# LayerNorm rows transposed by the DMA crossbar instead of TensorE, from the fifth tile on

## The chip, the cores and the metric

The kernel runs on one core of one Trainium2 chip. A core has five engines with a queue each: TensorE (PE, with its weight loads shown apart as PEld), VectorE (DVE), ScalarE (ACT), GpSimd (POOL) and SyncE (SP). SP computes nothing here: it issues every DMA of the kernel, in order, and 16 DMA engines carry them out. The metric is the device time of one execution in microseconds; lower is better.

## The reference

Two layer kinds alternate, each twice, on one sequence of 2048 rows of 512 (bf16). A is sliding-window attention with 32 heads of 16 and a window of 256; B is an MLP with an inner width of 1792.

```python
def _A_ref(x, wqkv, wo):
    H = 32; Dh = D // H; W = 256
    q, k, v = split((x @ wqkv))                    # heads of 16
    scores = einsum("bhqd,bhkd->bhqk", q, k) * (Dh ** -0.5)
    mask = (i - j >= 0) & (i - j < W)
    p = softmax(where(mask, scores, -1e9))
    return einsum("bhqk,bhkd->bhqd", p, v).reshape(B, S, D) @ wo

def _B_ref(x, w1, b1, w2, b2):
    return gelu(x @ w1 + b1) @ w2 + b2

x = x + _A_ref(_layernorm(x), A_wqkv, A_wo)
x = x + _B_ref(_layernorm(x), B_w1, B_b1, B_w2, B_b2)
x = x + _A_ref(_layernorm(x), A_wqkv, A_wo)
x = x + _B_ref(_layernorm(x), B_w1, B_b1, B_w2, B_b2)
```

The LayerNorm has no weights: it subtracts the row's mean and divides by the square root of the variance plus 1e-5.

## The kernel before, in words

The sequence is cut into 16 tiles of 128 rows. The two passes over the layers are numbered through: `tau` runs from 0 to 31, and tile `tau % 16` of the residual `X` stays in on-chip memory all the time. All weights are loaded once at the start. Two tiles make a block `b` of attention (16 blocks over both passes).

What happens to one block:

- `lnq(b)` takes the LayerNorm of its two tiles into `xnTA` (layer 0), transposed, so that the row's 512 channels lie on partitions, and projects Q. `kv(b)` projects K and V from the same `xnTA`. Both are planned ahead of the block's attention: `lnq` two blocks ahead, `kv` one.
- `attention(b)` makes 8 x 2 visits. A visit multiplies K and Q of four heads in four row groups of PE (line 643), takes the exponential on ACT from PSUM into `E` (656), and masks it on DVE or POOL (661, 669). After every second pair of visits the products with V are accumulated (699), evacuated into `OD` by DVE or ACT, and divided by the softmax denominator.
- The division goes through DMA: `Dc` collects the denominators out of `OD` (716), DVE takes the reciprocal `Rc` (719), `scr_r` stores it in DRAM (721), `Rn` reads it back broadcast to all rows (723), four copies move the odd heads inside `OD` (726), and POOL or DVE multiplies into `OT` (729, 732). All seven DMAs of such a round are issued by SP. There are 64 rounds.
- `outproj` multiplies by Wo, adds to `X` (562), and takes the LayerNorm of layer 1 into `xnTB`.
- `mlp(J)` serves a job of two or four tiles from `xnTB`. Six of 14 inner chunks are evacuated by DVE first (786) and put through the gelu in pairs (789); the other eight go through ACT straight from PSUM (798). Then W2 and the second residual follow. In the second pass each finished tile is stored to the output (811). A job is let in `GLAG` = 26 visits after its tiles' block.

`layernorm` (line 508) is where the change acts. DVE takes the statistics (515, 517), POOL the reciprocal root (519, 522), DVE writes `xn` (525). Then the rows have to be turned:

- as it is before: four PE transposes into one PSUM bank (537), and an evacuation into `xnTA` or `xnTB` by DVE (line 502 within `evac`) or ACT (line 504), whichever the planner finds free first;
- the other branch: one `dma_start_transpose` issued on SP (530), which writes `xnTA` or `xnTB` directly.

The order of the instructions on each engine is fixed when the program is built. `_Plan` (168) is a list scheduler: every operation has an engine or alternatives, a cost in ns, a priority and the data that it reads and writes; PSUM banks come from pools (`"o"` is banks 6 and 7, for projections, PV, transposes and most outputs). For a DMA the plan has two numbers, the time for which SP is busy issuing (`issue`) and the time to landing (`dur`); for the transposing DMA they are `TRI` = 500 and `TRD` = 4300 ns. `_Sched` (20) then emits the operations in that order with semaphore waits. DMAs use eight semaphores in turn, and each waits until the previous one on its semaphore has landed:

```python
        if dma:
            assert eng == "sp"
            counter = "spdma%d" % (self.dma_rr % self.N_DMA_SEMS)
            self.dma_rr += 1
            inc = 16
            prev = self.cnt_val[counter]
            if prev > 0:
                need(counter, prev)
```

Of the kernel before, what the change touches and what calls it, by code (L numbers as in the profile page):

```python
# [330 lines left out]
def bass_interleave_layers__sliding_block__dense_activation_gelu__prompt_kernel(  # L331
# [39 lines left out]
    GLAG = 26  # L371
    MP1, MP2, QP, KP = 5.0, 255.0, 110.0, 140.0
    PVLAG = 1
    NPT = 1000
    TRD, TRI = 4300.0, 500.0
    PG = 2
    PREP = 0.0
# [19 lines left out]
    with ExitStack() as kctx:  # L397
# [73 lines left out]
        def dma(fn, writes, reads=(), dur=2200.0, prio=0.0, issue=330.0):  # L471
            add("sp", fn, dur, reads=reads, writes=writes, prio=prio, dma=True, geo=issue)
# [35 lines left out]
        def layernorm(tau, layer, dst, dcol, dname, prio):  # L508
# [19 lines left out]
                reads=["X%d" % t, "mv%d" % k, "rs%d" % k], writes=["xn%d" % s], prio=prio)  # L528
            if NPT <= tau + 100 * layer:
                dma(lambda e, B: e.dma_start_transpose(dst[:, :, dcol : dcol + P], xn[:, s, :]),  # L530
# [342 lines left out]
```

## Time and profile before

| | |
|---|---|
| median of three runs | 560.25 us (557.84 to 560.73) |
| the profiled execution's own time | 560.25 us |
| its span in the profile | 558.5 us |
| granted TensorE clock, mean | 0.976 of full speed |
| PE busy | 497.5 us (89%) |
| ACT busy | 476.9 us (85%) |
| DVE busy | 386.7 us (69%) |
| POOL busy | 281.3 us (50%) |
| DMA engines busy, mean share (SP's queue) | 14.4% |

Busy is the time in which an engine carries out an instruction. Matmuls are pipelined and their ends are modelled, so PE's busy time reads higher than its real work. An operation in a group is written out<-in with its line; the idle time given with a group is that of its engine just before it, with what ended it. SPq stands for SP's instruction queue. The chain that ended last is followed back from the last instruction, at each step to what released it.

### The profile page before, as it was taken

How to read it: one execution, taken by the hardware profiler on the slowest of the kernel's cores; microseconds unless marked ns; L12 is line 12 of the kernel's file. 1: busy time of each engine (PE TensorE's matmuls, PEld its weight loads, DVE VectorE, ACT ScalarE, POOL GpSimd, SP SyncE). 2: the span in 40 equal slices, each digit the busy share in tenths (PEclk: the TensorE clock that was granted, in tenths of full speed). 3: DMA queues.
4: the chain of work that ended last, by engine and by line, in shares of the span. 5: the costliest groups of instructions: out<-in, count | busy, mean ns of one | idle time of the engine just before them, and what ended most of it. 6: DMA issues, size and time to landing. Idle time of an engine off the chain costs nothing.

```text
span 558.5 us, 12849 instructions
## 1 busy us (share of the span) xinstructions
PE 497.5 (89%) x5008; PEld 238.5 (43%) x5008; DVE 386.7 (69%) x769; ACT 476.9 (85%) x708; POOL 281.3 (50%) x470
## 2 busy tenths in 40 slices
PE   3885689999979999888999999899999999878997
PEld 2543245445434443434334443444434543333553
DVE  5899688696879567946588667986787666735131
ACT  2699789999979999977989999899997999887532
POOL 6467564483765465722576456743564356421010
PEclk9999679999979999999999999999999999989999
DMA  8901111010111101110111101110111001111100
GB/s 276 289 18 34 29 33 36 16 35 26 32 33 31 32 7 35 30 33 26 32 27 37 30 18 33 31 32 16 41 46 47 25 23 41 50 32 35 51 21 28
DMA packets 37103, 24.44 MB, mean 44 GB/s; under 512 B 16305, under 2 KB 36530, under 8 KB 37042
## 3 DMA queue, kind: packets, MB, share of 16 engines
q1 hardware_dynamic: 37042, 23.62, 14.4%
q8 instruction: 39, 0.64, 0.5%
q14 instruction: 22, 0.18, 0.1%
HBM read 16.26 MB, written 2.62 MB: 34 GB/s over the span
## 4 chain that ended last, share of the span: by engine, by line
PE 35%; ACT 25%; DMA 15%; DVE 12%; SPq 8%; issue 3%; POOL 2%; DVEq 0%; POOLq 0%
PE ps L553 26%; ACT E L656 17%; SPq L726 6%; DMA Dc<-OD 6%; DMA Rn<-scr_r 5%; PE ps L643 5%; DMA scr_r<-Rc 4%; PE ps L699 3%; DVE E L661 3%; ACT gT L798 2%; ACT gT L789 2%; PE ps L537 1%; DVE KT L597 1%; ACT OD L504 1%; DVE gT L786 1%
## 5 line engine op out<-in xcount | busy, mean ns | idle before, releaser
L656 ACT ACTIVATE E<-ps 128x768 bf16<-128x768 f32 (+2 forms) x512 | 357.3, 785 | 28.0 <-PE ps L643 25.9
L669 POOL TENSOR_SCALAR_AFFINE_SELECT E<-E 128x512 bf16<-128x512 bf16 x216 | 161.6, 749 | 138.1 <-ACT E L656 136.8
L661 DVE TENSOR_TENSOR E<-E,mask 128x512 bf16<-128x512 bf16 x195 | 99.0, 510 | 39.2 <-ACT E L656 37.5
L553 PE MATMUL ps<-W_sb,gT 128*128 128x512 bf16 x448 | 121.7, 382 | 0.0
L553 PE MATMUL ps<-xnTB,W_sb 128*128 128x512 bf16 (+1 forms) x560 | 116.4, 345 | 3.4 <-DVE gT L786 2.2
L643 PE MATMUL ps<-QT,KT 32*128 32x384 bf16 (+2 forms) x1024 | 86.9, 328 | 19.3 <-ACT E L656 18.4
L553 PE MATMUL ps<-xnTA,Wqkv_sb 128*128 128x256 bf16 x512 | 72.5, 282 | 2.8 <-ACT xnTA L504 0.7
L553 PEld LDWEIGHTS ps<-xnTB,W_sb 128*128 128x128 bf16 x560 | 51.0, 99 | 47.5 <-issue 6.1
L643 PEld LDWEIGHTS ps<-QT,KT 32*128 32x128 bf16 x1024 | 25.8, 91 | 96.4 <-ACT E L656 81.8
L562 DVE TENSOR_TENSOR X<-X,ps 128x512 bf16<-128x512 bf16 x64 | 43.3, 677 | 31.2 <-PE ps L553 30.8
L798 ACT ACTIVATE gT<-ps,b1T 128x512 bf16<-128x512 f32 (+1 forms) x92 | 48.4, 587 | 12.3 <-PE ps L553 12.3
L699 PE MATMUL ps<-E,Va 128*17 128x128 bf16 (+1 forms) x1920 | 53.6, 254 | 5.3 <-DVE E L661 1.2
L553 PEld LDWEIGHTS ps<-W_sb,gT 128*128 128x128 bf16 x448 | 37.2, 98 | 47.5 <-issue 19.8
L553 PEld LDWEIGHTS ps<-xnTA,Wqkv_sb 128*128 128x128 bf16 x512 | 45.9, 100 | 21.3 <-issue 4.8
L665 POOL TENSOR_SCALAR_AFFINE_SELECT E<-E 128x512 bf16<-128x512 bf16 x61 | 39.8, 654 | 20.4 <-ACT E L656 20.1
L699 PEld LDWEIGHTS ps<-E,Va 128*17 128x17 bf16 x1920 | 39.0, 93 | 25.3 <-issue 10.9
L729 POOL TENSOR_TENSOR OT<-OD,Rn 128x256 bf16<-128x256 f32 x35 | 26.6, 761 | 39.6 <-DMA Rn<-scr_r 37.0
L515 DVE BATCH_NORM_STATS2 stat<-X 128x6 f32<-128x512 bf16 x64 | 43.0, 678 | 0.7
L597 DVE TENSOR_TENSOR KT<-ps,parmask 128x1024 bf16<-128x1024 f32 x32 | 38.8, 1213 | 6.5 <-PE ps L553 6.3
L537 PE MATMUL ps<-ident,xn 128*128 128x128 bf16 x256 | 26.1, 228 | 18.5 <-DVE xn L525 13.3
L519 POOL TENSOR_SCALAR veps<-statmv 128x1 f32<-128x1 f32 x64 | 15.2, 240 | 53.2 <-DVE statmv L517 53.0
L522 POOL TENSOR_TENSOR rstd<-veps,mhalf 128x1 f32<-128x1 f32 x64 | 38.3, 600 | 3.3
(44 smaller groups left out, 408.0 us busy)
## 6 DMA issues: line engine op xcount, KB each, us to landing
Rn<-scr_r SPq DMA_DIRECT2D x64, 128.0 KB
OD<-OD SPq DMA_DIRECT2D x256, 16.0 KB
W_sb<-in_B_w_dram SPq DMA_DIRECT2D x2, 1792.0 KB
out_dram<-X SPq DMA_DIRECT2D x16, 128.0 KB
Wqkv_sb<-in_A_wqkv_dram SPq DMA_DIRECT2D x3, 512.0 KB
X<-in_A_x_dram SPq DMA_DIRECT2D x1, 1024.0 KB
Dc<-OD SPq DMA_DIRECT2D x64, 8.0 KB
scr_r<-Rc SPq DMA_DIRECT2D x64, 8.0 KB
```

The costliest lines, as they stand in the source:

```text
L515: add("dve", lambda e, B: e.bn_stats(stat6[:, k6, :], X[:, t, :]), 680, reads=["X%d" % t], writes=["st%d" % k6], prio=prio)
L522: add("pool", lambda e, B: e.tensor_tensor(out=rstd[:, k : k + 1], in0=veps[:, k : k + 1], in1=mhalf[:], op=ALU.pow), 590, reads=["ve%d" % ...
L553: r = e.matmul(ps[:, B[g][0], cols], lhsT, rhs, start=st, stop=sp)
L562: add("dve", lambda e, B: e.tensor_tensor(out=X[:, t, :], in0=X[:, t, :], in1=ps[:, B[g][0], :], op=ALU.add), d_psum(512), reads=["X%d" % ...
L597: add("dve", lambda e, B, g=g, i=i: e.tensor_tensor(out=KT[:, kb, :, 2 * i : 2 * i + 2, :].rearrange("p a c q -> p a (c q)"), in0=ps[:, B[ ...
L643: x = e.matmul(ps[:, bk[r], 0:N], KT[rows, kb, par, c, j * P : (j + 1) * P], QT[rows, c, q0 : q0 + N], start=True, stop=True)
L656: a = (add("act", lambda e, B, g=g, gi=gi: e.activation(E[:, es, 2 * gi : 2 * gi + 2, 0:N], ps[:, B[g][0] : B[g][0] + 2, 0:N], AF.Exp, sca ...
L661: add("dve", lambda e, B: e.tensor_tensor(out=E[:, es, :, 0:P], in0=E[:, es, :, 0:P], in1=mask01[:, None, 0, :].to_broadcast([P, RG, P]), ...
L665: alt=(("pool", lambda e, B: e.affine_select(E[:, es, :, 0:P], E[:, es, :, 0:P], [[0, RG], [1, P]], ALU.is_ge, 0.0, base=0, channel_multip ...
L669: add("pool", lambda e, B: e.affine_select(E[:, es, :, 2 * P : 3 * P], E[:, es, :, 2 * P : 3 * P], [[0, RG], [-1, P]], ALU.is_ge, 0.0, bas ...
L699: x = e.matmul(ps[32 * r : 32 * r + VW, B[g][0], par * 256 + q_lo * P : par * 256 + (q_hi + 1) * P], Va[:, (2 * b + k) % VR, h, :], E[:, e ...
L798: gelu_last[0] = add("act", lambda e, B, g=g, fc=fc: e.activation(gT[:, fc, 0:M], ps[:, B[g][0], 0:M], AF.Gelu_apprx_tanh, bias=b1T[:, fc ...
```

## The change

One constant: from `NPT` = 1000 to `NPT` = 4. It enters in line 529 alone.

```diff
@@ -371,7 +371,7 @@
     GLAG = 26
     MP1, MP2, QP, KP = 5.0, 255.0, 110.0, 140.0
     PVLAG = 1
-    NPT = 1000
+    NPT = 4
     TRD, TRI = 4300.0, 500.0
     PG = 2
     PREP = 0.0
```

The condition and its two branches, which stay as they are:

```python
            if NPT <= tau + 100 * layer:
                dma(lambda e, B: e.dma_start_transpose(dst[:, :, dcol : dcol + P], xn[:, s, :]),
                    [dname], reads=["xn%d" % s], prio=prio - 60, dur=TRD, issue=TRI)
            else:
                g = "tp%d" % k
                ...
                add("pe", tr, 4 * 56.0, reads=["xn%d" % s, "ident"], writes=["ps:" + g], prio=prio,
                    alloc=("o", [(g, 1)]), geo="f", war=[dname])
                evac(lambda B: dst[:, :, dcol : dcol + P],
                     ...
                     ["ps:" + g], [dname], prio, free=[g], two=True, kind="t", boot=True)
```

With 1000 the second branch is taken for every tile. With 4 the first four tiles of layer 0 keep it, and the other 28 of layer 0 and all 32 of layer 1 take the first. The plan is made anew with the other operations, so the order on every engine may differ.

## The prediction

> **What bounds the kernel now.** I read the engine totals first, then the slices, the chain that ended last, the groups of the touched lines, and last the waits of the DMA queue on SP.
>
> ```profile
> PE 497.5 (89%) x5008; PEld 238.5 (43%) x5008; DVE 386.7 (69%) x769; ACT 476.9 (85%) x708; POOL 281.3 (50%) x470
> PE   3885689999979999888999999899999999878997
> ACT  2699789999979999977989999899997999887532
> PE 35%; ACT 25%; DMA 15%; DVE 12%; SPq 8%; issue 3%; POOL 2%; DVEq 0%; POOLq 0%
> ```
>
> The first line is busy time and share, the next two are tenths in 40 slices of 14 us, the last is the chain of waits by engine. From slice 7 to slice 33 TensorE and ScalarE both stand at 8 or 9: two engines feed each other and neither is far from full. But 15 + 8 = 23% of the chain, 128 us, is neither: it is transfers and their issue on SP. They are the softmax denominators, 64 rounds of Dc out of OD, a reciprocal, scr_r, Rn and four OD copies. In the stretch from 500 to 531 us, where the last block ends, the chain is almost nothing else.
>
> ```profile
> L537 PE MATMUL ps<-ident,xn 128*128 128x128 bf16 x256 | 26.1, 228 | 18.5 <-DVE xn L525 13.3 <-DVE Va L502 1.6 <-ACT xnTA L504 1.2
> L504 ACT ACTIVATE xnTA<-ps 128x512 bf16<-128x512 bf16 x17 | 10.4, 617 | 7.9 <-PE ps L537 7.9
> L504 ACT ACTIVATE xnTB<-ps 128x512 bf16<-128x512 bf16 x8 | 4.8, 606 | 5.6 <-PE ps L537 5.5
> L502 DVE COPY xnTA<-ps 128x512 bf16<-128x512 bf16 x15 | 6.2, 416 | 4.1 <-PE ps L537 3.9
> L502 DVE COPY xnTB<-ps 128x512 bf16<-128x512 bf16 x24 | 10.0, 419 | 9.7 <-PE ps L537 9.6
> ```
>
> These five groups are the whole present transpose (busy us and mean ns, then idle before). The last view, the waits on SP's own queue, shows what the new transfers will meet:
>
> ```profile
> SPq L726 <- DMA Dc<-OD: 62.0, 50, 1.7
> SPq L127 <- DVE OD L502: 36.7, 10, 9.3
> SPq L127 <- ACT OD L504: 26.2, 6, 11.1
> SPq L127 <- DMA scr_r<-Rc: 16.3, 18, 2.1
> SPq L127 <- DMA Dc<-OD: 13.9, 10, 1.7
> SPq L723 <- DMA scr_r<-Rc: 8.2, 9, 2.2
> ```
>
> SP issues in order. Its instructions last 608 ns (Dc), 536 (scr_r), 647 (Rn) and 587 (each OD copy) at the median: 64 x (0.608 + 0.536 + 0.647 + 4 x 0.587) = 265 us, with the 16 stores of 0.367 us 271 us. It waits 62.0 + 16.3 + 13.9 + 8.2 = 100 us for transfers that it issued itself, and some 115 us for evacuations and other producers. Only this last part is slack.
>
> [...] The trace has 219 ns for one TensorE transpose (median), and four in a row take PE 0.22 to 0.40 us; it has no crossbar transfer. [...]
>
> **The change, part by part.** Line 529 becomes true for tau >= 4 in layer 0 (28 tiles) and for all 32 in layer 1: 60 of 64.
>
> Removed. On PE, 60 groups of four: 60 x 0.22 us = 13 us of pace, and L537 is 1.3% of the chain, 7 us. On ACT, 25 evacuations less some three of the first four tiles: 22 x 0.61 = 13.4 us. On DVE 38 x 0.418 = 15.9 us. The 60 allocations of PSUM banks 6 and 7 go too; waits for those banks (as PEld L537 behind Va, 3.2 us) are a few us at most. These savings run at the same time on three engines, so they don't add: the two full engines each lose 13 us. **I take 12 us of gain.** Both ends: 0, if the order waits elsewhere; 20, if DVE's free time also takes over some of the 31 OD evacuations of 0.6 us that ACT does.
>
> Added on SP: 60 transposes. Issue time isn't in the trace. The nearest row is a store of 0.367 us. [...] Lower end 0.5 us, what the plan is told (TRI). Upper end 4 us: W2's load with 1,792 rows took 1.87 us to issue, so (1.87 - 0.367) / (1,792 - 128) = 0.9 ns a row[...].
>
> Time on the rings: [...] I take 2 us. The landing then comes some 4 us after issue (small copies land in 1.8 to 2.1 us), against about 1 us on PE plus evacuation.
>
> What stands behind. Each transpose waits on SP for xn from DVE; a Dc, scr_r or Rn queued after it waits with it, and behind those wait the reciprocal (DVE already idles 21.2 us for Dc), OT on POOL and DVE (37.0 and 24.8 us for Rn) and the out-projection. The eight DMA semaphores are used in turn, so a transpose also holds up the eighth transfer after it. Of 1.2 us of issue about half falls into SP's waits for its own transfers (100 us, 1.7 per transpose) and is hidden; of 2 us on the rings about half meets a round under way. So 0.6 + 1.0 = 1.6 us of delay per transpose, one per round. A round takes 8.5 us (Dc issued at 209.24, Rn landed at 217.70), 64 rounds 544 us, of which 128 us lie on the chain: a share of 0.235. In the body, 56 x 1.6 x 0.235 = **21 us of loss**.
>
> At the tail there is no cover. Between 500 and 531 us every SP instruction is on the chain, and the transposes of tiles 28 and 29 (layer 1) fall there: 2 x (1.2 + 1) = 4.4 us. Those of 30 and 31 come after 531 us; from xn to xnTB is 540.95 - 538.23 = 2.7 us now, and would be 1.2 + 4 = 5 us: 2 us more. **6 us of loss.** Start: tiles 0 to 3 stay on PE; nothing. The LN of layer 0 runs two blocks ahead of use, and that of layer 1 26 visits before its MLP, so the 3 us of added latency itself is hidden except at the tail.
>
> Edits at nothing: VectorE's xn and the statistics stay. Consumers wait on DMA semaphores in place of ACT's or DVE's, one wait for another. The whole order is planned anew from the costs in the code, which I count as neutral, +-5 us.
>
> Sum: -12 + 21 + 6 = +15 us. The profiled execution took 560.25 us (span 558.5 and 1.75 around it), which is also the median of the three shown. So **575 us**.
>
> **Rivals.**
> 1. Cheap transposes, faster. If issue is 0.5 us and rings 0.5 us, nearly all falls into SP's 115 us of slack: 56 x 0.3 x 0.235 = 4 us, tail 3 us, gain 12 to 20 us: 547 to 555, I say 550. For it: both full engines get 13 us back. Against: 23% of the chain lies in the very queue that is loaded. It decides below about 0.7 us of delay per transpose, where 60 x 0.7 x 0.235 + 3 equals the gain of 12.
> 2. SP's queue becomes the bound, much slower. Slack of 115 us over 60 is 1.9 us each; with issue at 3 us, 60 x (3 - 1.9) = 66 us come out of the end, with the tail 640. [...] Against: the plan's 0.5 us.
> 3. A draw: losses equal the gain, 558 to 563.
> 4. That the switch does nothing is excluded: 60 tiles satisfy line 529, a condition that the old 1000 never met.
>
> **How the numbers follow.** Moderate loss (563 to 600) 0.50; SP-bound (600 and up) 0.13; draw 0.09; faster 0.28. A difference of 0.5%, 2.8 us, is about the least that a measurement of this kernel can tell from no change. Range 546 to 625: it takes in rival 1 almost whole and leaves the upper half of rival 2 out. The loss case alone would be 563 to 600.
>
> **What would show it.** PE L537 must fall to 16 instructions, xnTA/xnTB evacuations on ACT and DVE to four in all. The new SP line should show 1.2 us a piece and about 4 us to landing; 0.5 us speaks for rival 1, 3 us for rival 2. Right: idle of OT and Rc waiting for Rn and Dc grows above 62 and 21 us, and DMA plus SPq exceed 23% of the chain. Wrong: those waits stay, and ACT's busy time falls with the span. The prediction falls altogether if the landing is under 3 us.

## The result, and the profile after

The changed kernel takes 605.5 us in the median of four executions (602.0 to 607.3), the kernel before 560.5. The ratio, here and below of the mean times, is 1.078, with a 95% interval of 1.069 to 1.087. The forecast was slower, 575 us. The direction held and the 605.5 lies in the range, but the loss is 45 us where 15 were forecast, three times as much. It lies above the band of moderate loss that was held likeliest (563 to 600). The profiled execution took 602.0 us with a span of 600.3.

The page of the changed kernel, busy time by engine and three rows of the slices (PEclk is the granted TensorE clock in tenths of full speed):

```profile
PE 503.1 (84%) x4768; PEld 229.9 (38%) x4768; DVE 367.1 (61%) x729; ACT 466.2 (78%) x681; POOL 282.7 (47%) x477
PE   3786686988868889859998978989889889688997
ACT  2678585997987889966998969889787788868623
PEclk9985666998986999999999979999898999879999
```

The row PEclk of the kernel before:

```profile
PEclk9999679999979999999999999999999999989999
```

The work did leave the engines: ACT has 10.7 us and DVE 19.6 us less. PE has 240 instructions fewer and yet 5.6 us more busy time. In slice 7 both full engines fall, PE from 9 to 6 and ACT from 9 to 5, and the granted clock from 9 to 6. The clock was low before the change too, in slices 5 and 6; now it is low from slice 4 to 7 and again in slice 13.

The chain of waits of the changed kernel, by engine and by line:

```profile
PE 29%; DMA 23%; SPq 19%; ACT 12%; DVE 7%; POOL 5%; issue 3%; POOLq 0%; DVEq 0%
PE ps L553 23%; SPq L726 11%; ACT E L656 10%; DMA Dc<-OD 9%; DMA Rn<-scr_r 7%; DMA scr_r<-Rc 6%; SPq L530 4%; PE ps L699 3%; PE ps L643 3%; SPq L723 2%; DMA xnTA<-xn 2%; POOL OT L729 2%; POOL E L669 1%; SPq L721 1%; DVE KT L597 1%
```

DMA and SPq together were 23%, 128 us; they are now 42%, 252 us. Only 4% is the issue of the transposes themselves (L530) and 2% their landing: nearly all the rest is the old denominator rounds, longer on the path than before.

The new line by itself (minimum, median and maximum in ns), the waits on SP's queue that answer to those shown before, and the groups that wait for the rounds:

```profile
L530 SPq DMA_TRANSPOSE xnTB<-xn x32: 1192/1224/2113, 76.7 to 580.0; - x32
L530 SPq DMA_TRANSPOSE xnTA<-xn x28: 1192/1261/5523, 21.8 to 441.0; - x28
```

```profile
SPq L127 <- DMA Dc<-OD: 34.4, 30, 1.7
SPq L726 <- DMA Dc<-OD: 22.8, 18, 1.7
SPq L127 <- DMA scr_r<-Rc: 16.6, 19, 2.1
...
SPq L127 <- ACT OD L504: 12.2, 6, 7.3
SPq L723 <- DMA scr_r<-Rc: 11.6, 12, 3.0
```

```profile
L537 PE MATMUL ps<-ident,xn 128*128 128x128 bf16 x16 | 1.9, 263 | 9.2 <-DVE xn L525 8.6 <-DVE xnTA L502 0.6
L719 DVE RECIPROCAL Rc<-Dc 64x32 f32<-64x32 f32 x64 | 21.8, 340 | 45.2 <-DMA Dc<-OD 45.2
L729 POOL TENSOR_TENSOR OT<-OD,Rn 128x256 bf16<-128x256 f32 x47 | 35.8, 763 | 109.8 <-DMA Rn<-scr_r 83.1 <-DMA OD<-OD 15.0 <-DMA Dc<-OD 11.6
```

The wait of DVE for the same Rn:

```profile
DVE OT L732 <- DMA Rn<-scr_r: 24.3, 11, 4.5
```

The issue of 1.22 to 1.26 us is what was estimated. Some of SP's waits for evacuations shrank (26.2 to 12.2 us for ACT's OD): it comes later to work that is ready by then. Its waits for its own transfers fell only from 100 to 34.4 + 22.8 + 16.6 + 11.6 = 85 us. All its waits together fell from 249 to 217 us, so 32 of the 74 us of added issue were absorbed; the other 42 match the growth of the span. And DVE's idle time for Dc has doubled (21.2 to 45.2 us), POOL's for Rn more than doubled (37.0 to 83.1), while DVE's for Rn stayed (24.8 to 24.3).

One such place, from the chain of waits in order of time (start, length, what):

```profile
49.70 0.47 PE ps L643 x4
50.16 0.79 SPq L530
...
51.00 1.27 SPq L530
...
52.37 0.57 SPq L726
...
54.30 1.74 DMA scr_r<-Rc
56.05 0.65 SPq L723
...
63.66 2.74 DMA Rn<-scr_r
...
66.57 0.73 POOL OT L729
...
67.35 3.59 PE ps L553 x8
```

The same out-projection in the kernel before:

```profile
62.51 3.59 PE ps L553 x8
```

Two transposes go ahead of OD copies that are ready by then. Later Rn lands at 66.4, POOL multiplies, and PE, which had stood still for 1.96 us, starts the out-projection. Before the change PE waited 0.72 us for the same multiplication, and the same eight matmuls started 4.8 us earlier. They took 3.59 us there as well, and the granted clock was 0.50 in both stretches (62.51 to 66.10 us before, 67.35 to 70.94 after).

The start of the kernel lost time in another way. The first transpose was issued while the DMA engines still moved the loads of the start (347 GB/s from 22 to 24 us), and landed 7.79 us later:

```profile
21.82 7.79 DMA xnTA<-xn
```

The first four occupied SP for 10.9 us, and PE stood still for 3.2 us until the matmuls that need these rows began at 30.15.

### The profile page after: what moved, and what is told of

Its sections match the earlier page's. It is cut to its first block, busy times and chain, and to the rows that moved or that the text cites. A ratio compares the mean times of both kernels' runs of the same rounds, so it can differ in the third digit from the quotient of the medians.

```text
span 600.3 us, 12434 instructions
## 1 busy us (share of the span) xinstructions
PE 503.1 (84%) x4768; PEld 229.9 (38%) x4768; DVE 367.1 (61%) x729; ACT 466.2 (78%) x681; POOL 282.7 (47%) x477
## 2 busy tenths in 40 slices
DMA packets 69741, 32.28 MB, mean 54 GB/s; under 512 B 48945, under 2 KB 69170, under 8 KB 69682
## 4 chain that ended last, share of the span: by engine, by line
PE 29%; DMA 23%; SPq 19%; ACT 12%; DVE 7%; POOL 5%; issue 3%; POOLq 0%; DVEq 0%
PE ps L553 23%; SPq L726 11%; ACT E L656 10%; DMA Dc<-OD 9%; DMA Rn<-scr_r 7%; DMA scr_r<-Rc 6%; SPq L530 4%; PE ps L699 3%; PE ps L643 3%; SPq L723 2%; DMA xnTA<-xn 2%; POOL OT L729 2%; POOL E L669 1%; SPq L721 1%; DVE KT L597 1%
## 5 line engine op out<-in xcount | busy, mean ns | idle before, releaser
L669 POOL TENSOR_SCALAR_AFFINE_SELECT E<-E 128x512 bf16<-128x512 bf16 x216 | 158.8, 742 | 116.6 <-ACT E L656 115.9
L553 PE MATMUL ps<-W_sb,gT 128*128 128x512 bf16 x448 | 125.2, 395 | 0.0
L661 DVE TENSOR_TENSOR E<-E,mask 128x512 bf16<-128x512 bf16 x200 | 96.3, 484 | 45.5 <-ACT E L656 44.7
L643 PE MATMUL ps<-QT,KT 32*128 32x384 bf16 (+2 forms) x1024 | 91.3, 345 | 23.9 <-ACT E L656 22.8
L553 PE MATMUL ps<-xnTA,Wqkv_sb 128*128 128x256 bf16 x512 | 80.1, 307 | 9.4 <-DVE xn L525 3.2
L729 POOL TENSOR_TENSOR OT<-OD,Rn 128x256 bf16<-128x256 f32 x47 | 35.8, 763 | 109.8 <-DMA Rn<-scr_r 83.1
L643 PEld LDWEIGHTS ps<-QT,KT 32*128 32x128 bf16 x1024 | 26.1, 92 | 111.7 <-ACT E L656 90.6
L553 PEld LDWEIGHTS ps<-xnTA,Wqkv_sb 128*128 128x128 bf16 x512 | 50.0, 108 | 33.9 <-issue 12.0
L553 PEld LDWEIGHTS ps<-W_sb,gT 128*128 128x128 bf16 x448 | 38.0, 100 | 51.7 <-issue 24.3
L719 DVE RECIPROCAL Rc<-Dc 64x32 f32<-64x32 f32 x64 | 21.8, 340 | 45.2 <-DMA Dc<-OD 45.2
L525 DVE TENSOR_SCALAR xn<-X,statmv,rstd 128x512 bf16<-128x512 bf16 x64 | 30.3, 481 | 23.9 <-POOL rstd L522 17.8
L553 PE MATMUL ps<-Wo_sb,OT 128*128 128x512 bf16 x128 | 35.5, 409 | 10.5 <-POOL OT L729 7.0
L665 POOL TENSOR_SCALAR_AFFINE_SELECT E<-E 128x512 bf16<-128x512 bf16 x56 | 36.5, 654 | 12.4 <-ACT E L656 12.3
```

Of the source, the lines that this page charges most:

```text
L553: r = e.matmul(ps[:, B[g][0], cols], lhsT, rhs, start=st, stop=sp)
L643: x = e.matmul(ps[:, bk[r], 0:N], KT[rows, kb, par, c, j * P : (j + 1) * P], QT[rows, c, q0 : q0 + N], start=True, stop=True)
L661: add("dve", lambda e, B: e.tensor_tensor(out=E[:, es, :, 0:P], in0=E[:, es, :, 0:P], in1=mask01[:, None, 0, :].to_broadcast([P, RG, P]), ...
L669: add("pool", lambda e, B: e.affine_select(E[:, es, :, 2 * P : 3 * P], E[:, es, :, 2 * P : 3 * P], [[0, RG], [-1, P]], ALU.is_ge, 0.0, bas ...
L729: add("pool", lambda e, B: e.tensor_tensor(out=OT[:, bs, c, :], in0=OD[:, s, 0, :], in1=Rn[:, rs, :], op=ALU.mult), 750, reads=ods + ["Rn% ...
```

## The experiments

Four theories were set against each other. **Q**: the transposes' issue time delays the rounds in SP's in-order queue. **R**: their traffic does, on the DMA engines. **L**: the readers wait for rows that land late. **P**: the order that the plan makes is bad, because the plan has wrong prices.

### e1: the changed order without the transposes

In the emission loop, the 60 DMA operations are skipped and xnTB is zeroed once:

```diff
         for i in order:
+            if i in left_out:
+                continue
             nd = PL.nodes[i]
```

> The changed kernel in its own order, with its 60 transposes left out of the program: xnTB is filled with zeros once at the start and xnTA keeps the first tiles' values, so the numbers computed downstream are not the reference's; everything else is issued as in the changed kernel. Theory Q (the transposes' 1.2 us of issue on SP pushes the denominator rounds back, and that is the whole loss): the time falls to the kernel before less the relief of PE, ACT and DVE, 545 to 555 us. Theory P (the order planned for the changed kernel is bad by itself): it stays above 575 us. Theory L (the latency of the transposed rows holds their readers): also a fall to about 550, so Q and L are told apart by the next two runs.

Measured: 557.9 us, ratio 0.995 (0.992 to 0.997). The order alone isn't bad, so P in its plain form falls. The 60 transposes in this order cost 605.5 - 557.9 = 48 us. The relief of three engines in this order is worth 2 to 3 us. One reservation holds for e1 and for e6 below: part of their data are zeros or old values, and no run here tests whether the values alone move the clock.

### e2 and e3: transposes, or as much issue time, added to the kernel before

PE keeps transposing; after each xn of the same 60 tiles SP gets an extra DMA into a scratch tile.

```diff
+                S_.op("sp", lambda e, k=k, q=q: e.dma_start_transpose(trash[:, q], xn[:, k, :]),
+                      reads=[x], writes=["trash%d" % q], dma=True)
```

> The kernel before, in its own order, with 60 crossbar transposes added on SP after the same xn tiles, into a scratch tile that nobody reads; PE still transposes. Theory Q: rounds are delayed as in the changed kernel, 590 to 615 us, although no reader ever waits for a transposed row. Theory L: no reader waits, so at most 565 us. Theory P: the order is that of before, so at most 570 us.

Measured: 596.2 us, 1.065 (1.060 to 1.070). In e3 two copies of 16 KB stand in its place:

> The kernel before, with two copies of 16 rows of 1 KB (0.58 us of issue each, 1.2 us together) on SP in place of each added transpose of the run beside it. Theory Q says that only the issue time counts: within 8 us of the run with added transposes. Theory R [...]: at most 570 us, since these copies move 32 KB and hardly occupy the engines.

Measured: 592.0 us, 1.057 (1.050 to 1.063). The added line of each run (e2, then e3):

```profile
L850 SPq DMA_TRANSPOSE trash<-xn x60: 1188/1214/6896, 20.4 to 573.7; - x60
```

```profile
L851 SPq DMA_DIRECT2D trash<-xn x120: 507/580/5635, 19.7 to 571.8; - x120
```

With 1.2 us of issue a tile either way, both runs lose nearly alike, 36 and 32 us, and their intervals overlap, although the transposes keep the DMA engines busier (21.1% against 15.0%, by SP's queue). So L isn't needed for a loss of this size (nobody reads these rows), and R explains some 4 us of it. What counts is time in SP's queue. In the changed kernel L has a small part, the wait at the start shown above: PE and its weight loads waited directly for transposed rows 1.2 and 5.0 us in all.

### e4 and e5: the plan told the transposes' true price

```diff
-    TRD, TRI = 4300.0, 500.0
+    TRD, TRI = 2600.0, 1250.0     # e4
+    TRD, TRI = 4300.0, 1250.0     # e5
```

> The changed kernel with the plan told what the trace shows: 1250 ns of issue in place of 500, 2600 ns to landing in place of 4300. Theory P (the plan's wrong price is what makes the order bad): 570 us or less. Theory Q: the same 75 us of issue stand in the same queue, so 590 to 605 us, a few us better at most.

> The changed kernel with one number of the plan changed: issue 1250 ns in place of 500, the 4300 ns to landing left. If the issue price alone made the difference of the run told both numbers (577 us against 605), this gives 572 to 584 us. If the shorter landing of 2600 ns had done it, this stays at 595 us or above.

Measured: 577.4 us, 1.031 (1.026 to 1.036), and 571.6 us, 1.019 (1.014 to 1.024). Not one transpose was taken away, and 28 to 34 us came back; theory Q as I had put it for e4 (590 to 605) was wrong. The load in the queue costs most where the plan doesn't know of it: SP then reaches its instructions later than the plan placed them. This lag is called slip below. The issue price alone does it; the shorter landing price brings nothing (e4 is 6 us slower than e5).

### e6: transposes at no cost

e1 with `TRD, TRI = 1.0, 1.0`, so that the plan, too, counts on none.

> The changed kernel with the transposes planned at no cost and left out of the program (xnTB filled with zeros once, so the numbers downstream are not the reference's): what PE, ACT and DVE can give when their 13, 13 and 16 us are taken off and the order is planned for it. The prediction's gain term was 12 us: 545 to 551 us. If the relief is worth little because the rounds on SP, and not the full engines, set the pace, it stays at 555 to 560 us.

Measured: 550.0 us, 0.982 (0.976 to 0.989). Once the order is planned for it, the relief is worth 11 us; the prediction had 12. In the changed kernel's order (e1) it was 2 to 3.

### e7 and e8: the rounds' prices put right as well

The plan was wrong about the rounds already before the change. Prices in ns as the trace shows them, with the gap after each instruction:

```diff
-  dur=2200.0, issue=580.0     +  dur=2200.0, issue=650.0     # Dc
-  dur=2000.0, issue=490.0     +  dur=2000.0, issue=580.0     # scr_r
-  dur=3200.0, issue=580.0     +  dur=3200.0, issue=690.0     # Rn
-  dur=2200.0, issue=350.0     +  dur=2200.0, issue=630.0     # OD, four a round
```

> The kernel before, with the plan's SP issue prices of the denominator rounds set to what the trace shows with the gap after each: Dc 650, scr_r 580, Rn 690, each OD copy 630 ns (580, 490, 580, 350 before). Four copies are 1.1 us too cheap per round in the old plan, as a transpose is 0.7 us too cheap. If wrong issue prices are what makes the queue slip behind its plan, this is faster than before, 535 to 553 us. If the wrong price matters only beside the transposes, it is 556 to 564 us.

> The changed kernel with the same prices of the rounds and 1300 ns for the transposes' issue (4300 ns to landing left). If the remaining loss of the run told only the transposes' price (577 against 560 us) is the queue's true load, this stays within 8 us of it, 568 to 582 us; if it is still slip against the plan, it falls to 562 us or less.

Measured: e7 (kernel before) 546.9 us, 0.976 (0.969 to 0.982); e8 (changed kernel, with TRI = 1300) 541.6 us, 0.965 (0.960 to 0.971). Both beat both kernels of this study. The chain of waits of e7, then of e8:

```profile
PE 57%; ACT 29%; DVE 7%; issue 3%; POOL 2%; DMA 1%; SPq 1%; POOLq 0%; DVEq 0%
```

```profile
PE 53%; ACT 19%; DVE 11%; DMA 6%; SPq 5%; issue 3%; POOL 3%; DVEq 0%; POOLq 0%
```

The 23% of the kernel before, read in the prediction as a load that was simply there, was mostly slip against the plan: with right prices it is 2%. With 60 transposes in the queue it is 11%, in place of 42%. A share of the chain is no saving, though: DMA and SPq gave up some 117 us of it from the kernel before to e7, and the time fell by 14, because other work took their place on the chain.

### e9: only the rounds priced

The changed kernel with the four prices of e7 and 500 ns left for a transpose.

> The changed kernel with only the rounds' four prices set to what the trace shows, and 500 ns left for a transpose. Of the four combinations three are known: neither price right 605 us, the transposes' alone 572, both 542. If slip of the queue against its plan is what costs, and each microsecond of it counts alike (0.75 us a transpose, about 1.4 us a round), this lies between, 558 to 578 us. If the transposes' price alone matters once they are there, it stays at 590 us or above.

Measured: 561.7 us, 1.002 (1.000 to 1.005), within what was expected. This completes the table. Unpriced time is what the plan leaves out on SP: 60 x 0.8 = 48 us for transposes (1.3 us with its gap against 0.5), 64 x (0.07 + 0.09 + 0.11 + 4 x 0.28) = 89 us for rounds.

| SP time that the plan doesn't know | changed kernel | kernel before |
|---|---|---|
| none | 541.6 (e8) | 546.9 (e7) |
| 48 us, transposes | 561.7 (e9) | |
| 89 us, rounds | 571.6 (e5) | 560.5 |
| 137 us, both | 605.5 | |

In the changed kernel the first 48 us cost 20, the 89 us 30, and the 48 us on top of the 89 cost 34. In the kernel before, with a shorter queue, 89 us cost 14. In this table slip costs more the fuller the queue is and the more there is of it, and each microsecond left out costs between 0.15 and 0.7.

### e10 and e11: the two priced kernels again, side by side

> The same kernel as the run with both prices right, in five rounds beside the next one: 537 to 546 us. With the same plan prices on both sides, the crossbar is then worth 3 to 8 us over the PE transposes, if what was seen once holds.

> The same kernel as the run of the kernel before with the rounds' prices right, in five rounds: 543 to 550 us. If the two intervals lie apart, the change is a gain under a plan with right prices and a loss under one with wrong ones; if they overlap, it is a draw under right prices.

Measured: 543.2 us, 0.968 (0.963 to 0.973), and 546.3 us, 0.974 (0.969 to 0.979). The intervals overlap, which the expectation for e11 called a draw. But both are ratios to the same kernel before, and the two priced kernels can be compared directly. In both series the changed kernel is ahead, by 5 and by 3 us. All four executions of e8 (538.7 to 544.6) lie below all four of e7 (545.1 to 551.2), and over both series, ten executions each, the means are 542.8 and 547.0. So with right prices the changed kernel is faster by about 4 us, 0.8%. That is less than the 6 us that the landing price alone moved (e4, e5), so it isn't shown that the crossbar, and not the order made for it, is what gains.

### e12: all prices a quarter too high

```diff
-    TRD, TRI = 4300.0, 500.0
+    TRD, TRI = 4300.0, 1625.0     # and 810, 725, 860, 790 for the rounds
```

> The changed kernel with all five issue prices a quarter above what the trace shows (Dc 810, scr_r 725, Rn 860, OD 790, transpose 1625 ns). If only slip counts (work that comes later than planned), slack in the plan costs little and this stays at 538 to 548 us. If the right price itself is the optimum, it is worse than both right prices by more than 6 us.

Measured: 552.9 us, 0.985 (0.979 to 0.991), 10 us above the right prices. Some 91 us of SP time are priced that aren't there (60 x 0.325 + 64 x 1.115). The chain of e12:

```profile
PE 49%; ACT 38%; DVE 5%; DMA 4%; issue 2%; POOL 1%; SPq 1%; DVEq 0%; POOLq 0%
```

SP has nearly left the path, and still the kernel is slower; that the plan holds work back or orders it worse is the likely reason, and no run tells which. Prices too low by about the same amount cost more: 30 us for the 89 us of e5, against 10.

## Why the prediction was off, step by step

**The direction and the path held.** The signs that the prediction named came: the idle time of OT for Rn went from 62 to 83.1 + 24.3 = 107 us, that of Rc for Dc from 21 to 45, and DMA with SPq from 23% to 42% of the chain.

**The issue time held.** The 1.2 us was my own estimate, which the trace of before, without a crossbar transfer, couldn't show; 1.22 and 1.26 were measured at the median. The upper bound of 4 us is passed by one transpose alone, at the start (5.52 us). The 60 transposes bring 69,741 - 37,103 = 32,638 packets more, 544 each.

**Ring time and landing were too long.** I took 2 us and 4 us; the 2 us was likewise my own estimate, shown by no trace. In the body of the changed kernel, and of e4, transposes on the chain landed 2.5 us after their issue began (in e4 2.5 to 2.9):

```profile
418.92 2.48 DMA xnTA<-xn
```

With 1.26 us of issue taken off, 1.2 us of this are left, an estimate from this one transfer. The prediction named "under 3 us" as what would make it fall altogether. It didn't: the bulk of the loss doesn't come from the landing (e2, e3). Only at the start, which was put at nothing, did a landing of 7.8 us hold up PE.

**The step that failed is "The whole order is planned anew from the costs in the code, which I count as neutral, +-5 us".** The order isn't bad in itself (e1); it is bad for transposes that take 1.2 us where it leaves room for 0.5. I had both numbers side by side, and the four OD copies at 350 against 587 ns in the trace, and used the plan's only as a lower bound for the cost. With the transposes' price right, 34 us of the changed kernel's time go (605.5 against e5's 571.6), and with the rounds' as well 64 us (e8's 541.6). The order on each engine is fixed, so PE, DVE and POOL can stand in front of the one instruction whose input slipped, even with other work ready.

**The loss was mis-sized with it.** The sum was -12 + 21 + 6 = 15 us. Measured in the changed order (e1) it is -3 + 48 = 45 us, so 0.8 us a transpose where 27 / 60 = 0.45 were forecast. Added to the order of before, the same 60 cost 36 us (e2). The share of 0.235 was taken from a chain whose 23% were mostly slip already, and was kept constant, while it rose to 42%. The parts came out the other way round. Of the 1.6 us of delay, 0.6 stood for issue and 1.0 for the rings, 8 and 13 us of the 21; e3 shows 32 us for issue alone, and e2 only 4 more for everything else. That the sum missed by less than its parts is luck. And half of the issue time was to vanish in SP's waits for its own transfers, 36 us; these fell by 15.

**The gain of 12 us was right only for another order.** It is 11 us when planned for (e6), 2 to 3 us in this order (e1). That freed PE and ACT time becomes waiting time where SP's rounds set the pace is the likely reason; no run isolates it.

**The tail's 6 us did not come.** From the last exponential's start to the end of the span it was 558.5 - 516.3 = 42.2 us and is 600.3 - 559.5 = 40.8. Of the last four transposes the first two were issued at 549.07 and 551.09, while the last block's exponentials still ran. The reading that every SP instruction between 500 and 531 us is on the chain was too strong: from 509 to 514 the chain runs over DVE, PE and ACT. So was the reading that both engines stand at 8 or 9 from slice 7 to 33: PE has one 7 there and ACT four.

**The rivals.** The time of 605.5 falls into the band of the full queue (600 and up), but not by its mechanism, an issue time of 3 us: SP issues 265 + 6 + 60 x 1.24 = 345 us and waits 217 in a span of 600. The draw and the cheap transposes were judged against this change as it stands, and there they are wrong; under right prices (e8, e10) the changed kernel, at 541.6 and 543.2, lies below the cheap rival's 550.

**What stays open.** How much of the 45 us is the lower TensorE clock (0.920 against 0.976 in the mean), and how much the stalls themselves; no run here separates the two. How far the time moves by chance when a plan comes out differently; no run changed a price that shouldn't matter. And whether the 4 us between the two priced kernels belong to the crossbar.

## What to carry to other kernels

In a kernel whose order is written from a cost table, compare that table with the trace before anything else: time that the table leaves out on an in-order queue delays instructions that are already placed. Here 137 us left out cost 64, while the transposes' 74 us of issue, once in the plan, cost nothing net of their relief (e8 against e7). A change that adds to such a queue is judged only after its price is right; here the same change is an 8% loss with wrong prices and a gain of under 1% with right ones. A queue's share in the chain of waits can be slip and not load, and one run with corrected prices tells which.

## What the runs showed of the hardware

In the stretches shown here the granted clock fell with short gaps in front of the matmuls, at most 1.96 us after the change (56 to 72 us) and 1.06 us before it (46 to 64 us). Stretches of the changed kernel (columns: stretch, length, busy us of PE, PEld, DVE, ACT and POOL with instructions, granted clock, DMA share, GB/s):

```profile
56.00:60.00 4.00, 2.49 (x18) 1.04 (x15) 1.67 (x4) 2.86 (x4) 1.68 (x4) 0.78 0.13 39
60.00:64.00 4.00, 2.64 (x45) 1.59 (x46) 2.62 (x7) 2.78 (x6) 3.44 (x5) 0.65 0.10 23
64.00:68.00 4.00, 2.04 (x11) 0.74 (x10) 2.53 (x4) 2.21 (x3) 1.66 (x3) 0.50 0.12 37
68.00:72.00 4.00, 4.00 (x43) 1.47 (x41) 2.05 (x4) 0.56 (x1) 0.84 (x2) 0.57 0.07 16
```

Two of the same stretches of the kernel before (busy time of ACT alone, then granted clock, DMA share and GB/s):

```profile
56.00:60.00 4.00, 3.67 (x6) 0.66 0.07 14
60.00:64.00 4.00, 2.94 (x4) 0.50 0.15 43
```

In these 16 us of the changed kernel the longest gap in front of a matmul is 1.96 us, and PE is busy for half to two thirds of the first three stretches; the clock goes down to 0.50, and the fourth stretch, with PE busy throughout, runs at 0.57. In the kernel before it goes down to 0.50 at 60 to 64 us as well, after gaps of at most 1.06 us from 46 us on, so this fall isn't the change's doing. The change makes it longer: from 28 to 112 us, in three stretches of 28, the clock is 0.73, 0.62 and 0.80, against 1.00, 0.70 and 1.00 before. Over the whole span the clock is 0.920, against 0.976 before, and the matmuls that both kernels share were busy 503.1 - 1.9 = 501.2 us against 497.5 - 26.1 = 471.4.

A crossbar transpose of 128 rows of 512 out of on-chip memory takes 1.2 us of SP's time, as much as two small copies (0.58 us each in e3), and lands in 2.5 us in the body, hardly later than Dc with its 8 KB (1.81 and 2.33 us on the chain of the kernel before, at 514 and 521 us). Beside the load at the start the issue took up to 5.5 us and the landing 7.8.
